# Attention scores made for two key chunks at a time, with the product of the high parts on half the rows

## The chip, the cores and the metric

The kernel runs on one core of one Trainium2 chip. The metric is device time in microseconds (us), the median of the runs of one program; lower is better. All engines of the core work at once: PE is TensorE (matmul), PEld its weight load, DVE is VectorE, ACT is ScalarE, SP the queue that issues the DMAs.

## The reference

Three layers follow each other: an attention with squared ReLU in place of a softmax, a channel mix, and a squared ReLU MLP. The change touches the first alone, in the product of z with itself:

```python
def _attn_ref(u, v, z):                       # u, v: 4 x 3072 x 256, z: 4 x 3072 x 64
    scale = 1.0 / S
    scores = scale * np.matmul(z, z.transpose(0, 2, 1))
    attn = np.maximum(scores, 0.0) ** 2
    out = np.matmul(attn, v)
    return (u * out).astype(np.float32)
```

All inputs are fp32.

## The kernel before

**Numbers in two parts.** Matmuls take fp32r operands. Each fp32 operand is cut into a high part (hi, a rounded copy) and a low part (lo, what is left), and a product is built from three terms, hi by hi, lo by hi and hi by lo, that add up in one PSUM bank.

**z.** z has 64 columns, so its hi and lo parts fit side by side on the 128 partitions. For each batch b and each group g of 512 positions there are two tiles in `zz`: `zhl[b, g]` holds hi on rows 0 to 63 and lo on rows 64 to 127, `zlh[b, g]` holds lo on rows 0 to 63 and hi on rows 64 to 127 (L271 to L275).

**Tiling.** A block n is one batch (4) and one group `ib` of 512 queries (6 of a batch), 24 blocks in all. A step s of a block is one chunk of 128 keys (24 chunks, 4 of a group g). For each step `scores(s)` makes a tile of 128 keys by 512 queries, and `attend(s)` multiplies it by v: six matmuls (L379, L380, L383) that add up over the 24 steps into two PSUM banks. Scores are symmetric: where g < ib the tile comes, turned, from an earlier block by way of DRAM (`turned`, loaded to `mixed`, L336 and L338; taken up by ACT L346 and DVE L347) and no score matmul is issued. So blocks with ib = 0, 1, ... 5 make 24, 20, ... 4 score chunks: 84 in a batch, 336 in all.

**One computed score chunk.** Two matmuls (L351, L352), each over all 128 rows, fill one PSUM bank `sps`: `zhl` by `zhl` gives hi by hi plus lo by lo, `zlh` by `zhl` gives lo by hi plus hi by lo. ACT then applies ReLU (L162, this frees the bank) and the square (L163); hi is made on DVE (L358) or ACT (L356), lo on DVE (L361), and where g > ib DVE transposes the tile for a later block (`turn`, L322), which SP stores.

**Order.** The order is the program's own (nothing is rescheduled). At step s the loop runs what is due by the table `todo` (loads, z and v splits, conversions of weights), then makes scores ahead up to a lead that grows from 4 to 7 steps, then issues `attend(s)`. The pool `ps_w` has four PSUM banks, so the bank of a chunk is the bank of the fourth chunk before it. Each step of the main stretch on PE is thus two score matmuls and six matmuls with v.

Of the kernel before, what the change touches and what calls it, by code (L numbers as in the profile page):

```python
# [7 lines left out]
F32 = mybir.dt.float32  # L8
# [7 lines left out]
P = 128  # L16
Q = 32
T = 512
# [3 lines left out]
def tile_relu2_attention__rwkv_channel_mix__relu2_mlp(  # L22
# [18 lines left out]
    nc = tc.nc  # L41
    B, S, D = u.shape
    DQ = z.shape[2]
# [25 lines left out]
    ps_w = ctx.enter_context(tc.tile_pool(name="ps_w", bufs=4, space=PSUM))  # L69
# [86 lines left out]
    def parts(pool, tag, bufs):  # L156
        return [pool.tile([P, T], F32R, tag=tag + h, name=tag + h, bufs=bufs) for h in ("hi", "lo")]

    def relu2(ps, scale):

        a = el.tile([P, T], F32, tag="a", name="a")
        nc.scalar.activation(out=a, in_=ps, func=AF.Relu, scale=scale)  # L162
        nc.scalar.activation(out=a, in_=a, func=AF.Square)  # L163
        return a
# [77 lines left out]
    def attention():  # L242
        with ExitStack() as st:
# [5 lines left out]
            z_raw, zT, zz, zhl, zlh, vhl, uT = {}, {}, {}, {}, {}, {}, {}  # L249
# [47 lines left out]
                uT[n, d] = io.tile([P, T], F32, tag=f"uT{d}", name="uT", bufs=1)  # L297
                nc.vector.transpose(uT[n, d], raws.pop(("u", n, d)))

            at, acc, ready, staged, late = {}, {}, {}, {}, []  # L300

# [2 lines left out]
            def chunk(s):  # L306

                n, jc = divmod(s, NJ)
                if n % NB == NB - 1:
                    jc = (jc - G) % NJ  # L310
                return n, n // NB, n % NB, jc // G, jc % G
# [6 lines left out]
            def turn(a, i, j, c):  # L318
                if c == 0:
                    staged[i, j] = io.tile([P, R, G, G, Q], F32, tag="turn", name="turn")  # L320
                t, s = staged[i, j], spread[i, j]
                nc.vector.transpose(t[:, :, :, c, :], a.rearrange("x (m r q) -> x q m r" if s else "x (m q r) -> x q m r",  # L322
                                                                  m=G, q=R))
                if c == G - 1:
                    to = turned[i, j]
                    nc.sync.dma_start(out=to if s else to.rearrange("q x f -> x q f"),
                                      in_=t.rearrange("x q m c k -> x q (m c k)"))
# [12 lines left out]
            def scores(s):  # L340
                n, b, ib, g, c = chunk(s)
                if g < ib:
                    a = ready[n, g][:, :, c].rearrange("y p c k -> y c p k")
                    hi, lo = at[s] = parts(*pools["hidden"])
                    hi_v, lo_v = (t.rearrange("y (c p k) -> y c p k", c=G, k=Q) for t in (hi, lo))
                    nc.scalar.copy(hi_v, a)  # L346
                    finish(lambda: nc.vector.tensor_tensor(out=lo_v, in0=a, in1=hi_v, op=ALU.subtract))  # L347
                    return
                cs = slice(c * P, (c + 1) * P)
                ps = ps_w.tile([P, T], F32, tag="w", name="sps")  # L350
                nc.tensor.matmul(ps, lhsT=zhl[b, g][:, cs], rhs=zhl[b, ib], start=True, stop=False)  # L351
                nc.tensor.matmul(ps, lhsT=zlh[b, g][:, cs], rhs=zhl[b, ib], start=False, stop=True)  # L352
                a = relu2(ps, 1.0 / S)
                hi, lo = at[s] = parts(*pools["hidden"])
                if g > ib and s % 3 < 2:
                    nc.scalar.copy(hi, a)  # L356
                else:
                    nc.vector.tensor_copy(hi, a)  # L358
                if g > ib:
                    turn(a, ib, g, c)  # L360
                finish(lambda: nc.vector.tensor_tensor(out=lo, in0=a, in1=hi, op=ALU.subtract))  # L361

            def finish(f=None):

                if late:
                    late.pop()()
                if f:
                    late.append(f)
# [29 lines left out]
            for b in range(1, B):  # L398
                end = b * NB * NJ
                for g in range(NG):  # L400
                    s = end - (46, 44)[g >= NG - 2] + 6 * g
# [3 lines left out]
                    s = end - NJ + G + 5 * g  # L405
# [13 lines left out]
            for n in range(NBLK):  # L419
                s = n * NJ  # L420
# [6 lines left out]
            for n in range(NBLK - 1):  # L427
                b, ib = divmod(n, NB)
                for g in range(ib):
                    need, stored = n * NJ + (g + ib // (NB - 1)) * G - LEAD, (b * NB + g) * NJ + ib * G + G - 1 - FIRST  # L430
                    s = max(need - EARLY, stored + 1, freed[-3] if len(freed) > 2 else 0, taken)
# [37 lines left out]
            s = n_steps - NJ  # L469
# [23 lines left out]
            for s in range(-FIRST, n_steps + 1):  # L493
                for f, a in todo.pop(s, ()):
                    f(*a)
                if made == n_steps:
                    finish()
                while made < min(n_steps, s + 1 + min(LEAD, FIRST + max(0, s - 2 * NJ) // NJ)):
                    scores(made)
                    made += 1  # L500
                if 0 <= s < n_steps:
                    attend(s)
# [320 lines left out]
    with tc.manual_schedule():  # L823
        attention()
        hp = ctx.enter_context(tc.tile_pool(name="hp", bufs=1, reuse_waits="tile"))
        w3 = ctx.enter_context(tc.tile_pool(name="w3", bufs=1, reuse_waits="tile"))
        pools["ops", 0] = ctx.enter_context(tc.tile_pool(name="ops0", bufs=1, reuse_waits="tile"))
        for q in range(2):
            w_tiles(w3, q)
        channel_mix()  # L830
        mlp()
# [29 lines left out]
```

## Time and profile before

| | |
|---|---|
| median of 3 runs | 2539.12 us (2537.5 to 2540.91) |
| the profiled execution, its own time | 2538.36 us |
| its span, first to last instruction | 2536.6 us |
| granted TensorE clock, mean | 0.998 |

The profile is of one execution. "Busy" of PE is the union of its matmuls, whose ends are modelled: a matmul is shown from its start for 0.39 us, though the next may start sooner. So a pace is read from starts. PEld shows the weight loads, one ahead of each matmul. The attention fills the first 980 us of the span; the other two layers, which the change leaves alone, the rest.

### The profile page before, as it was taken

How to read it: one execution, taken by the hardware profiler on the slowest of the kernel's cores; microseconds unless marked ns; L12 is line 12 of the kernel's file. 1: busy time of each engine (PE TensorE's matmuls, PEld its weight loads, DVE VectorE, ACT ScalarE, POOL GpSimd, SP SyncE). 2: the span in 40 equal slices, each digit the busy share in tenths (PEclk: the TensorE clock that was granted, in tenths of full speed). 3: DMA queues.
4: the chain of work that ended last, by engine and by line, in shares of the span. 5: the costliest groups of instructions: out<-in, count | busy, mean ns of one | idle time of the engine just before them, and what ended most of it. 6: DMA issues, size and time to landing. Idle time of an engine off the chain costs nothing.

```text
span 2536.6 us, 31670 instructions
## 1 busy us (share of the span) xinstructions
PE 2513.0 (99%) x11040; PEld 2072.7 (82%) x11040; DVE 2007.8 (79%) x3382; ACT 1664.6 (66%) x2879; POOL 0.2 (0%) x4
## 2 busy tenths in 40 slices
PE   7999999999999999999999999999999999999998
PEld 5888888888888888888888888788888888888887
DVE  8898988988988986777776677877777777777776
ACT  8766876786687654555555566666666666666665
POOL 0000000000000000000000000000000000000000
PEclk9999999999999999999999999999999999999999
DMA  7678677787886770111111112100110011100101
GB/s 189 173 201 202 195 200 186 201 229 185 198 232 185 211 188 26 58 59 42 59 34 50 47 54 67 28 23 17 34 34 17 17 34 34 26 26 17 34 17 17
DMA packets 311121, 243.79 MB, mean 96 GB/s; under 512 B 211377, under 2 KB 229809, under 8 KB 307889
## 3 DMA queue, kind: packets, MB, share of 16 engines
q1 hardware_dynamic: 308848, 241.25, 35.6%
q8 instruction: 86, 1.41, 0.2%
q10 hardware_dynamic: 2112, 0.52, 0.1%
q14 instruction: 75, 0.61, 0.1%
HBM read 136.86 MB, written 104.86 MB: 95 GB/s over the span
## 4 chain that ended last, share of the span: by engine, by line
PE 92%; DVE 3%; ACT 2%; DMA 1%; issue 1%; SPq 1%; DVEq 0%; ACTq 0%
PE ups L652 16%; PE ups L208 13%; PE v L379 9%; PE v L383 9%; PE v L380 9%; PE v L668 6%; PE v L669 6%; PE v L670 6%; PE v L234 3%; PE v L230 3%; PE v L231 3%; PE sps L352 3%; PE sps L351 3%; DMA mixed<-turned 1%; ACT s L692 0%
## 5 line engine op out<-in xcount | busy, mean ns | idle before, releaser
L380 PE MATMUL v<-ahi,vhl 128*128 128x512 f32 x1152 | 448.8, 390 | 2.6 <-DVE vhl L286 2.6
L379 PE MATMUL v<-ahi,vhl 128*128 128x512 f32 x1152 | 449.1, 390 | 1.1 <-ACT ahi L346 1.1
L689 ACT ACTIVATE s<-s 128x512 f32<-128x512 f32 x288 | 181.2, 629 | 333.5 <-DVE s L684 333.4
L383 PE MATMUL v<-alo,vhl 128*128 128x512 f32 x1152 | 356.1, 390 | 4.0 <-DVE alo L361 3.9
L163 ACT ACTIVATE a<-a 128x512 f32<-128x512 f32 x528 | 333.9, 632 | 16.8
L652 PE MATMUL ups<-d,win 128*128 128x512 f32 x1152 | 323.7, 389 | 0.0
L668 PE MATMUL v<-hhi,wout 128*128 128x512 f32 x768 | 299.3, 390 | 0.7 <-ACT hhi L697 0.6
L670 PE MATMUL v<-hlo,wout 128*128 128x512 f32 x768 | 299.3, 390 | 0.5 <-DVE hlo L703 0.5
L669 PE MATMUL v<-hhi,wout 128*128 128x512 f32 x768 | 298.8, 389 | 0.0
L208 PE MATMUL ups<-mixed,wk 128*128 128x512 f32 x1152 | 291.8, 389 | 0.0
L703 DVE TENSOR_TENSOR hlo<-s,hhi 128x512 fp32r<-128x512 f32 x384 | 264.6, 689 | 21.7 <-ACT hhi L697 9.5
L162 ACT ACTIVATE a<-ups 128x512 f32<-128x512 f32 x192 | 114.8, 598 | 235.9 <-PE ups L208 207.9
L383 PEld LDWEIGHTS v<-alo,vhl 128*128 128x128 f32 x1152 | 215.5, 188 | 52.3 <-DVE alo L361 7.9
L380 PEld LDWEIGHTS v<-ahi,vhl 128*128 128x128 f32 x1152 | 216.6, 188 | 48.3 <-DVE vhl L286 3.4
L379 PEld LDWEIGHTS v<-ahi,vhl 128*128 128x128 f32 x1152 | 216.7, 188 | 47.1 <-ACT ahi L346 2.0
L652 PEld LDWEIGHTS ups<-d,win 128*128 128x128 f32 x1152 | 216.3, 188 | 44.9
L208 PEld LDWEIGHTS ups<-mixed,wk 128*128 128x128 f32 x1152 | 216.2, 188 | 44.9
L162 ACT ACTIVATE a<-sps 128x512 f32<-128x512 f32 x336 | 199.2, 593 | 81.5 <-PE sps L352 73.7
L652 PE MATMUL ups<-b,win 128*128 128x512 f32 x864 | 242.9, 389 | 0.0
L692 ACT ACTIVATE s<-s 128x512 f32<-128x512 f32 x384 | 231.2, 627 | 6.1
L322 DVE STREAM_TRANSPOSE turn<-a 128x512 f32<-128x512 f32 x240 | 207.2, 864 | 18.3 <-ACT a L163 16.8
L361 DVE TENSOR_TENSOR alo<-a,ahi 128x512 fp32r<-128x512 f32 x336 | 220.3, 660 | 0.0
(103 smaller groups left out, 3918.0 us busy)
## 6 DMA issues: line engine op xcount, KB each, us to landing
turned<-turn SPq DMA_DIRECT2D x60, 1024.0 KB, 5.1
mixed<-turned SPq DMA_DIRECT2D x220, 256.0 KB, 5.4
raw<-in_v_dram SPq DMA_DIRECT2D x24, 512.0 KB, 4.7
u<-in_u_dram SPq DMA_DIRECT2D x192, 64.0 KB, 4.3
xT<-uT SPq DMA_DIRECT2D x48, 256.0 KB, 2.2
x2d<-xo SPq DMA_DIRECT2D x48, 256.0 KB, 2.2
x<-x2d SPq DMA_DIRECT2D x12, 1024.0 KB, 4.8
out_dram<-y SPq DMA_DIRECT2D x92, 128.0 KB, 2.9
```

What stands on the lines that cost most here:

```text
L162: nc.scalar.activation(out=a, in_=ps, func=AF.Relu, scale=scale)
L163: nc.scalar.activation(out=a, in_=a, func=AF.Square)
L208: nc.tensor.matmul(ps, lhsT=lhs(h, c, f), rhs=rhs[:, m, c, :], start=k == 0, stop=k == 3 * ND - 1)
L379: nc.tensor.matmul(acc[n][d], lhsT=vt[:, 0, c, ds_], rhs=hi, start=first, stop=False)
L380: nc.tensor.matmul(acc[n][d], lhsT=vt[:, 1, c, ds_], rhs=hi, start=False, stop=False)
L383: nc.tensor.matmul(acc[n][d], lhsT=vt[:, 0, c, ds_], rhs=lo, start=False, stop=last)
L652: nc.tensor.matmul(ps, lhsT=win[q][:, h, r, w], rhs=x(y), start=first and m == 0, stop=m == 2, skip_group_check=not first)
L668: nc.tensor.matmul(acc[p, b][d], lhsT=w[:, 0, c, ds_], rhs=hi, start=first, stop=False)
L669: nc.tensor.matmul(acc[p, b][d], lhsT=w[:, 1, c, ds_], rhs=hi, start=False, stop=False)
L670: nc.tensor.matmul(acc[p, b][d], lhsT=w[:, 0, c, ds_], rhs=lo, start=False, stop=last)
L692: nc.scalar.activation(out=tmp[g, c], in_=tmp[g, c], func=AF.Square)
L703: nc.vector.tensor_tensor(out=lo, in0=tmp.pop((g, c)), in1=hi, op=ALU.subtract)
```

## The change

`scores` issues the matmuls of two neighbouring key chunks together, at the even chunk. It takes two PSUM banks and issues four matmuls: for each of the two chunks the cross terms over all 128 rows (`zlh` by `zhl`, L352 of the changed kernel), then for the even chunk hi by hi from rows 0 to 63 (of `zhl`), and for the odd chunk hi by hi from rows 64 to 127 (of `zlh`), both L355. These last two have 64 rows each, and lie on the two halves of the array. The term lo by lo is no longer computed. At the odd chunk no matmul is issued. Everything after the matmuls is as before.

```diff
-            at, acc, ready, staged, late = {}, {}, {}, {}, []
+            at, acc, ready, staged, sps, late = {}, {}, {}, {}, {}, []
...
-                cs = slice(c * P, (c + 1) * P)
-                ps = ps_w.tile([P, T], F32, tag="w", name="sps")
-                nc.tensor.matmul(ps, lhsT=zhl[b, g][:, cs], rhs=zhl[b, ib], start=True, stop=False)
-                nc.tensor.matmul(ps, lhsT=zlh[b, g][:, cs], rhs=zhl[b, ib], start=False, stop=True)
+                if c % 2 == 0:
+                    for k in range(2):
+                        sps[s + k] = ps_w.tile([P, T], F32, tag="w", name="sps")
+                        nc.tensor.matmul(sps[s + k], lhsT=zlh[b, g][:, (c + k) * P:(c + k + 1) * P], rhs=zhl[b, ib],
+                                         start=True, stop=False)
+                    for k, (rows, t) in enumerate(((slice(0, DQ), zhl), (slice(DQ, P), zlh))):
+                        nc.tensor.matmul(sps[s + k], lhsT=t[b, g][rows, (c + k) * P:(c + k + 1) * P],
+                                         rhs=t[b, ib][rows], start=False, stop=True)
+                ps = sps.pop(s)
                 a = relu2(ps, 1.0 / S)
```

On PE, two steps early in the second batch stand in this order before (names: `sps` are the score banks, `v_` or `v0`, `v1` the two banks that add up the product with v, `ahi` and `alo` the parts of a score chunk; numbers are buffers):

```order
L351 MATMUL sps_2860<-zz_1988,zz_2195 128x512 [waits Activation_49]
L352 MATMUL sps_2860<-zz_1988,zz_2195 128x512
L379 MATMUL v0_2730<-ahi_2724,vhl_2532 128x512
L380 MATMUL v0_2730<-ahi_2724,vhl_2532 128x512
L379 MATMUL v1_2731<-ahi_2724,vhl_2532 128x512
L380 MATMUL v1_2731<-ahi_2724,vhl_2532 128x512
L383 MATMUL v0_2730<-alo_2725,vhl_2532 128x512
L383 MATMUL v1_2731<-alo_2725,vhl_2532 128x512
L351 MATMUL sps_2878<-zz_1988,zz_2195 128x512 [waits Activation_49]
L352 MATMUL sps_2878<-zz_1988,zz_2195 128x512
```

After it, the same place on PE (the even chunk's bank has the same name, the odd one's is now `sps_2862`; L384, L385 and L388 are the matmuls with v):

```order
L352 MATMUL sps_2860<-zz_1988,zz_2195 128x512 [waits Activation_49]
L352 MATMUL sps_2862<-zz_1988,zz_2195 128x512 [waits Activation_49]
L355 MATMUL sps_2860<-zz_1988,zz_2195 128x512
L355 MATMUL sps_2862<-zz_1988,zz_2195 128x512
L384 MATMUL v0_2730<-ahi_2724,vhl_2532 128x512
L385 MATMUL v0_2730<-ahi_2724,vhl_2532 128x512
L384 MATMUL v1_2731<-ahi_2724,vhl_2532 128x512
L385 MATMUL v1_2731<-ahi_2724,vhl_2532 128x512
L388 MATMUL v0_2730<-alo_2725,vhl_2532 128x512
L388 MATMUL v1_2731<-alo_2725,vhl_2532 128x512
```

The odd chunk's two matmuls have moved ahead of the even step's six with v, and its wait for ACT (a free bank) with them. The number of matmuls is the same, and the order of the instructions on DVE, ACT and SP has not changed.

## Rows read from the trace of the kernel before

**Rows 1.** The page: span; busy us (share) xinstructions of each engine.

```profile
span 2536.6 us, 31670 instructions
PE 2513.0 (99%) x11040; PEld 2072.7 (82%) x11040; DVE 2007.8 (79%) x3382; ACT 1664.6 (66%) x2879; POOL 0.2 (0%) x4
```

**Rows 2.** Timeline of PE in one step (start us, us, instruction).

```profile
502.24 0.39 PE L351 MATMUL sps<-zz 128*128 128x512 f32 x1
502.46 0.39 PE L352 MATMUL sps<-zz 128*128 128x512 f32 x1
502.69 0.39 PE L379 MATMUL v<-ahi,vhl 128*128 128x512 f32 x1
...
504.05 0.39 PE L351 MATMUL sps<-zz 128*128 128x512 f32 x1
```

**Rows 3.** Timeline of PEld, the weight loads, in the same step.

```profile
502.24 0.19 PEld L352 LDWEIGHTS sps<-zz 128*128 128x128 f32 x1
502.46 0.19 PEld L379 LDWEIGHTS v<-ahi,vhl 128*128 128x128 f32 x1
```

**Rows 4.** What PE, then PEld waited for until 980 us (us, times, longest).

```profile
PE v L383 <- DVE alo L361: 3.9, 7, 0.9
PE v L379 <- ACT ahi L346: 1.1, 2, 0.7
...
PEld v L383 <- DVE alo L361: 7.9, 10, 1.3
PEld v L379 <- ACT ahi L346: 2.0, 2, 1.1
```

**Rows 5.** Stretches: PE, PEld, DVE, ACT, POOL busy us (x), PEclk, DMA share, GB/s.

```profile
12.00:65.20 53.20, 46.60 (x186) 34.77 (x185) 48.58 (x84) 46.48 (x81) 0.00 (x0) 0.97 0.79 204
65.20:106.40 41.20, 41.20 (x183) 34.14 (x182) 34.46 (x62) 32.16 (x55) 0.00 (x0) 1.00 0.71 194
259.70:301.40 41.70, 41.70 (x185) 34.55 (x184) 39.54 (x72) 37.18 (x65) 0.00 (x0) 1.00 0.85 240
301.40:341.30 39.90, 39.90 (x177) 33.04 (x176) 33.29 (x60) 31.03 (x53) 0.00 (x0) 1.00 0.68 191
419.30:457.40 38.10, 38.10 (x170) 31.56 (x169) 33.98 (x62) 24.08 (x42) 0.00 (x0) 1.00 0.82 198
```

**Rows 6.** The source line L352 (xcount: ns min/median/max, first and last start us).

```profile
L352 PE MATMUL sps<-zz x336: 387/389/628, 8.2 to 920.3; 128*128 128x512 f32 x168
```

**Rows 7.** Timeline of PEld, then of PE, just after a wait with the array empty.

```profile
15.27 0.19 PEld L380 LDWEIGHTS v<-ahi,vhl 128*128 128x128 f32 x1 [3.37 <-DVE vhl L286]
15.38 0.19 PEld L379 LDWEIGHTS v<-ahi,vhl 128*128 128x128 f32 x1
...
15.27 0.50 PE L380 MATMUL v<-ahi,vhl 128*128 128x512 f32 x1 [2.65 <-DVE vhl L286]
15.61 0.39 PE L379 MATMUL v<-ahi,vhl 128*128 128x512 f32 x1
```

**Rows 8.** Timeline of ACT: the four ReLUs ahead of 505 us, and the next.

```profile
498.34 0.59 ACT L162 ACTIVATE a<-sps 128x512 f32<-128x512 f32 x1
...
499.50 0.58 ACT L162 ACTIVATE a<-sps 128x512 f32<-128x512 f32 x1
...
501.35 0.60 ACT L162 ACTIVATE a<-sps 128x512 f32<-128x512 f32 x1
...
503.70 0.59 ACT L162 ACTIVATE a<-sps 128x512 f32<-128x512 f32 x1
...
504.86 0.58 ACT L162 ACTIVATE a<-sps 128x512 f32<-128x512 f32 x1
```

**Rows 9.** What ACT waited for until 925 us (us, times, longest).

```profile
ACT a L162 <- PE sps L352: 73.7, 101, 4.4
...
ACT ahi L346 <- DMA mixed<-turned: 31.8, 6, 6.0
```

**Rows 10.** Stretches of 20 us: columns as in rows 5; the last but one is DMA share.

```profile
220.00:240.00 20.00, 20.00 (x90) 16.57 (x89) 17.75 (x31) 11.11 (x20) 0.00 (x0) 1.00 1.05 255
240.00:260.00 20.00, 19.34 (x86) 15.70 (x85) 16.00 (x30) 15.35 (x28) 0.00 (x0) 1.00 0.62 175
```

## The prediction

> **What bounds the kernel now.** The page first: PE is busy 2513 of 2536.6 us, DVE 2008, ACT 1665 [rows 1]. A busy PE need not be a full one, since the ends of matmuls are modelled, so the second view is the timeline of PE in one step. There a matmul starts every 0.23 us, and the eight of the step take 504.05 - 502.24 = 1.81 us, or 0.226 us each [rows 2]. Each weight load starts with the matmul before the one it serves, and is over (0.19 us) before the slot is [rows 3]: loads cost nothing here. The third view is what PE waited for. In the whole attention that is a few us: 7.9 us of its loads for lo on DVE, ten times, and 2.0 us for hi made from turned scores, twice [rows 4]. So PE sets the time, matmul by matmul, at 0.226 us each, and what is taken from PE there is taken from the end, as long as DVE and the DMAs keep up. How far they can is the fourth view, the stretches: a block that begins a batch (ib = 0) has DVE busy 39.5 of 41.7 us, the block after it 33.3 of 39.9, a late one 34.0 of 38.1 [rows 5]. The very first block is another matter: PE is busy 46.6 of 53.2 us there and DVE 48.6, so PE is not what it waits for.
>
> **The change part by part.**
>
> *Matmuls.* There are 336 score chunks [rows 6], so 168 pairs. A pair has four matmuls before and after. Before, they take four slots: 4 x 0.226 = 0.905 us. After, the first two (cross terms, 128 rows) are of the kind that the trace shows: two slots. The other two have 64 rows each, and no matmul of before has less than 128 [rows 6]. They read different rows of SBUF, hold their weights in different rows of the array, and write different banks. If they stream at the same time, the second costs only what it starts late, and that I call d. Its lower bound is 0: nothing else between them is shared. The upper bound of an overlap comes from the weight loads, which share a path. With the array empty a load starts at 15.27 and the next at 15.38 [rows 7], so one load holds the path for 0.11 us. Both loads (0.22 us) just fit into the slot of the second cross matmul, if the second load may run before the first half matmul starts: d = 0. If it starts only with that matmul, as every load does in rows 3, then d = 0.11. The trace has no row between the two, so I take the middle, d = 0.055 us, and keep both ends. A pair then saves 0.226 - 0.055 = 0.171 us.
>
> The Trainium skill speaks on this: "TensorE: Matmul & The Clock Gate", Part 3, The mechanism, says that loads for other row groups are pulled ahead of matmuls, and that matmuls on different row groups start about 4 ns apart. No run here shows it; with 0.004 us for d the sum below would be 2508 us, an estimate.
>
> *Sum.* The 12 pairs of the first block are counted at nothing, since DVE and ACT set its pace [rows 5]. 156 pairs x 0.171 = 26.7 us. From this goes what DVE takes back: in the three later blocks with ib = 0, 12 pairs x 0.171 = 2.1 us bring PE from 41.7 to 39.6 us, and DVE is busy for 39.5 of them [rows 5]; with so little room lo will be late now and then, and I count a third, 0.7 us a block, 2.1 us. And what the DMAs take back: PE already waited twice for turned scores [rows 4], behind ACT, which waited 6.0 us for one such load [rows 9], after a stretch in which the DMA engines were full (share 1.05, then 0.62) [rows 10]. A PE that arrives earlier waits longer there; I count 1.0 us for the four batches. So 26.7 - 2.1 - 1.0 = 23.6 us. The profiled execution has 2538.4 us, so 2514.8; the median of the runs lies 0.8 us above it, so 2516 us. With d = 0 and nothing taken back it is 156 x 0.226 = 35.3 us and 2504, with d = 0.11 it is 156 x 0.116 - 3.1 = 15.0 us and 2524.
>
> *The moved matmuls.* The odd chunk's cross matmul now stands a step ahead, so its bank has to be free a step (1.81 us) earlier. The chunk whose first matmul starts at 504.05 [rows 2] writes the bank that the ReLU from 499.50 to 500.08 freed, four chunks before its own [rows 8]: 3.97 us of room, of which 1.81 - 0.23 = 1.6 go. Behind a PE that waits here the six matmuls with v would queue, and behind them everything; with 2.4 us left I count nothing. The even chunk's ReLU can start one slot (0.23 us) later than now, as its bank is complete with the third matmul in place of the second; the odd one's can start more than a us earlier. ACT waited 73.7 us for scores [rows 9] and is not what bounds; hi and lo of a chunk have four to seven steps until they are used. No cost. The six matmuls with v of the even step start two slots later against their scores, those of the odd step as before: more room for DVE, not less. DVE, ACT and SP do the same work in the same order.
>
> **The rivals.**
>
> *The array has to run empty between matmuls of different depth (slower).* Each pair goes from 128 rows to 64 and back. If the first matmul of the other depth has to wait until the one before has ended, it starts 0.389 us after it [rows 6], not 0.226: 0.163 more, twice a pair. A pair then takes 0.226 + 0.389 + 0.055 + 0.389 = 1.059 us against 0.905, so 0.154 x 168 = 25.9 us more: 2565. If the weight load also has to wait for the empty array, 0.11 more at each switch [rows 7]: 0.374 x 168 = 62.8, 2602. If it is only the load that is no longer hidden, 0.226 + 0.336 + 0.055 + 0.336 = 0.953, 8 us more, 2547. The point from which it decides is 0.171 / 2 = 0.086 us a switch: with more than that the change loses. For it speaks that nothing in the trace shows such a switch, so that nothing shows it free; against it, that in rows 3 and 7 a load never waits for a matmul to end, only for it to start. The Trainium skill has this rule: "TensorEngine Tiling (Array Packing)", Key Properties, says that switching the tiling mode drains TensorE. It gives no price, and no run here shows it.
>
> *The two halves don't run at the same time.* Then d is a whole slot, 0.226, a pair takes what it took, and only the order has changed: 2539, within some us. This is the case in which the change does not do what it says. For it speaks that no two matmuls of before start less than a slot apart.
>
> *The gain is there but DVE or the DMAs take most of it.* In the blocks with ib > 0 that rows 5 show, DVE has 4 to 7 us of room in 38 to 41, and the change takes at most 10 pairs x 0.171 = 1.7 there. For most of the gain to go, DVE would have to be late in all blocks: 2525 to 2533. Unlikely.
>
> **How the numbers follow.** Two runs of this kernel can be told apart from about 0.2% on, 5 us. Forecast, overlap, with 2503 to 2524 as its own range and 2516 as its value: 0.52. Gain mostly taken back: 0.04. No overlap, or a small cost at the switches that eats the gain, 2534 to 2544: 0.13. Slower by the switches, 2545 to 2602: 0.31. So faster 0.56, same 0.13, slower 0.31. Cases of both signs hold much of the chance, so the range is wide: from 2503, below which I leave 0.02, to 2568, above which lies somewhat less than half of the slower case, 0.14.
>
> **What would show it.** In the changed kernel's timeline, the two starts of L355 of one pair: 0 to 0.11 us apart if the halves overlap, 0.23 if they don't. The start of the first L355 after the second L352, and of the next matmul with v after the second L355: 0.23 us each if a switch is free, 0.3 to 0.5 if the array runs empty. The stretch of the attention should end near 980 - 24 = 956 us, and the rest should keep its 1557 us. PE's waits for lo on DVE (7.9 us now) should grow by a few us and no more, and PE should not wait for ACT at L352. The forecast is wrong if the switches cost 0.09 us or more each, or if the second L355 starts a slot after the first.

## The result and the profile after

The change made the kernel slower: 2568.16 us (median of 4 runs, 2567.88 to 2569.05) against 2539.13 us before (4 runs, 2537.5 to 2540.91). The ratio is 1.0115, with a 95% interval of 1.0097 to 1.0132, so 25 to 34 us more. The forecast was 2516 us, faster, with a range up to 2568: wrong in its sign, and just outside its range.

The page of the changed kernel, beside [rows 1]: PE is busy 34 us longer, DVE and ACT are busy as long as before.

```profile
span 2566.3 us, 31723 instructions
PE 2547.4 (99%) x11040; PEld 2029.0 (79%) x11040; DVE 2006.8 (78%) x3382; ACT 1665.5 (65%) x2879; POOL 0.2 (0%) x4
```

Where the time came in is told by the last matmul with v of the attention. Its source line, in the kernel before and in the changed one (name xcount: ns min/median/max, first to last start):

```profile
L383 PE MATMUL v<-alo,vhl x1152: 387/389/628, 16.2 to 980.2; 128*128 128x512 f32 x192
```

```profile
L388 PE MATMUL v<-alo,vhl x1152: 387/390/628, 16.1 to 1009.4; 128*128 128x512 f32 x192
```

The attention ends 29.2 us later, nearly all of the 29.7 us by which the span is longer; what follows takes 2566.3 - 1009.4 = 1556.9 us, against 2536.6 - 980.2 = 1556.4 before. Now one pair of chunks in the changed kernel, the timeline of PE (the L352 row holds both cross matmuls, the L355 row both matmuls of 64 rows):

```profile
504.95 0.61 PE L352 MATMUL sps<-zz 128*128 128x512 f32 x2
505.49 0.50 PE L355 MATMUL sps<-zz 64*128 64x512 f32 x2
505.92 0.50 PE L384 MATMUL v<-ahi,vhl 128*128 128x512 f32 x1
506.26 0.39 PE L385 MATMUL v<-ahi,vhl 128*128 128x512 f32 x1
506.49 0.40 PE L384 MATMUL v<-ahi,vhl 128*128 128x512 f32 x1
```

Two matmuls merged into one row are shown from the start of the first to the modelled end of the last, so a pair a slot apart is 0.226 + 0.39 = 0.61 long (the L352 row). A matmul that finds the array empty is recorded from its weight load on, and is then 0.50 long instead of 0.39; [rows 7] has one such too. The L355 row is 0.50 long for two matmuls: they start together. By single records (each instruction of the trace by itself) it is 0.003 to 0.004 us from the first start to the second, in 168 of 168 pairs. So two matmuls do go in one slot. But look at what is around them. From the start of the first cross matmul (504.95) to the second matmul with v (506.26) it is 1.31 us. Before, the same stretch held four score matmuls and one with v, five slots of 0.226, 1.13 us [rows 2]. One slot fewer, and 0.18 us longer. The loads of the same stretch, timeline of PEld:

```profile
504.72 0.41 PEld L352 LDWEIGHTS sps<-zz 128*128 128x128 f32 x2
505.49 0.19 PEld L355 LDWEIGHTS sps<-zz 64*128 64x128 f32 x2 [0.35 <-issue]
505.92 0.19 PEld L384 LDWEIGHTS v<-ahi,vhl 128*128 128x128 f32 x1 [0.25 <-issue]
506.03 0.19 PEld L385 LDWEIGHTS v<-ahi,vhl 128*128 128x128 f32 x1
```

In [rows 3] each load starts with the matmul before the one it serves. Here the loads of L355 should start with the second cross matmul, at 504.95 + 0.226 = 505.18. They start at 505.49, by single records 0.317 after the second cross matmul, which is a slot and another 0.09. In 165 of the 168 pairs it is 0.317 to 0.327 us. No semaphore held them, the profile says ("issue"). Only then does the load itself run, with nothing streaming: 0.11 us, as the distance of the next two loads shows (506.03 - 505.92). The same stands at the way back: L384's load starts 505.92 - 505.49 = 0.43 us after that of L355, which is 0.11 for the load, 0.226 for the slot, 0.09 again; and the matmul after it follows after 0.34, a slot and 0.11. So a change of depth costs 0.09 + 0.11 = 0.20 us, and a pair has two: 0.40, less the one slot saved, 0.226, is 0.18 us up to the second matmul with v.

The Trainium skill has the rule, "TensorEngine Tiling (Array Packing)", Key Properties: changing the tiling mode drains TensorE. The trace agrees, and puts the price beside it that the page doesn't give. That the 0.09 us are the emptying is the reading by this rule; the trace shows the delay alone.

0.18 us times 168 pairs is 30 us, near the 29.0 measured, but two parts of this sum are off and cancel. By single records five more slots behind each visit take 0.229 to 0.235 us at the median, together 0.02 us a pair; why is open. So a later block with ten pairs takes 43.74 us instead of 41.71, one with eight 41.52 instead of 39.89 (last matmul with v to last matmul with v): 0.203 us a pair. And the first block, whose pace PE doesn't set, is no longer than before: its last matmul with v starts at 63.8 us, before at 64.5. So 156 pairs x 0.203 = 31.7 us, less 0.7 in the first block, less 1.8 by which PE's waits for lo have shrunk (3.9 us in [rows 4], 2.1 now): 29.2, which is what the attention lost.

What PEld, then PE, waited for until 1150 us shows both sides of the visits in sums (us, times, longest), and that the pressure on DVE has not grown: PEld waits 6.9 us for lo, against 7.9 in [rows 4]:

```profile
PEld sps L355 <- issue: 59.9, 168, 0.7
...
PEld v L384 <- issue: 39.3, 160, 0.4
...
PEld v L388 <- DVE alo L366: 6.9, 12, 1.1
...
PE v L388 <- DVE alo L366: 2.1, 5, 0.7
```

### The profile page after: what moved, and what is told of

The parts are those of the page before. It is cut to its first block, busy times and chain, and to the rows that moved or that the text cites. A ratio compares the mean times of both kernels' runs of the same rounds, so it can differ in the third digit from the quotient of the medians.

```text
span 2566.3 us, 31723 instructions
## 1 busy us (share of the span) xinstructions
PE 2547.4 (99%) x11040; PEld 2029.0 (79%) x11040; DVE 2006.8 (78%) x3382; ACT 1665.5 (65%) x2879; POOL 0.2 (0%) x4
## 4 chain that ended last, share of the span: by engine, by line
PE 95%; DVE 2%; ACT 1%; DMA 1%; issue 0%; SPq 0%; DVEq 0%; ACTq 0%
PE ups L657 17%; PE ups L208 13%; PE v L384 11%; PE v L388 10%; PE v L385 10%; PE v L673 6%; PE v L675 6%; PE v L674 6%; PE v L231 3%; PE v L234 3%; PE v L230 3%; PE sps L352 3%; PE sps L355 3%; DMA zn<-in_z_dram 0%; DVE hlo L708 0%
## 5 line engine op out<-in xcount | busy, mean ns | idle before, releaser
L384 PE MATMUL v<-ahi,vhl 128*128 128x512 f32 x1152 | 468.5, 407 | 0.0
L385 PE MATMUL v<-ahi,vhl 128*128 128x512 f32 x1152 | 451.4, 392 | 0.2 <-DVE vhl L286 0.2
L388 PE MATMUL v<-alo,vhl 128*128 128x512 f32 x1152 | 357.8, 392 | 2.4 <-DVE alo L366 2.1
L384 PEld LDWEIGHTS v<-ahi,vhl 128*128 128x128 f32 x1152 | 216.7, 188 | 81.0 <-issue 39.3
L388 PEld LDWEIGHTS v<-alo,vhl 128*128 128x128 f32 x1152 | 215.7, 188 | 52.3 <-DVE alo L366 6.9
L385 PEld LDWEIGHTS v<-ahi,vhl 128*128 128x128 f32 x1152 | 217.2, 189 | 40.7 <-DVE vhl L286 0.7
```

Of the source, the lines that this page charges most:

```text
L384: nc.tensor.matmul(acc[n][d], lhsT=vt[:, 0, c, ds_], rhs=hi, start=first, stop=False)
L385: nc.tensor.matmul(acc[n][d], lhsT=vt[:, 1, c, ds_], rhs=hi, start=False, stop=False)
L388: nc.tensor.matmul(acc[n][d], lhsT=vt[:, 0, c, ds_], rhs=lo, start=False, stop=last)
```

## The experiments

The theory is the one just read: what costs is the *change* of depth, twice a pair, 0.09 us in which nothing starts and a load of 0.11 us that nothing hides. Its rivals: the new order of the matmuls (the odd chunk's brought ahead) costs the time; or the matmul of 64 rows itself does, wherever it stands.

### The order alone

Pairs and order as in the changed kernel, but hi by hi over all 128 rows again:

```diff
-                    for k, (rows, t) in enumerate(((slice(0, DQ), zhl), (slice(DQ, P), zlh))):
-                        nc.tensor.matmul(sps[s + k], lhsT=t[b, g][rows, (c + k) * P:(c + k + 1) * P],
-                                         rhs=t[b, ib][rows], start=False, stop=True)
+                    for k in range(2):
+                        nc.tensor.matmul(sps[s + k], lhsT=zhl[b, g][:, (c + k) * P:(c + k + 1) * P], rhs=zhl[b, ib],
+                                         start=False, stop=True)
```

> The pairing and the order of the changed kernel, but hi by hi over all 128 rows again (with lo by lo, as before), so no matmul has 64 rows. Theory (switch): the loss comes from going from 128 rows to 64 and back, about 0.2 us each time, twice a pair; without 64-row matmuls the time is that of before, 2539 within 5 us. Rival (order): the loss comes from the two banks taken at once and the odd chunk's matmuls moved a step ahead; then about 2568. Rival (half-depth matmul): a 64-row matmul is slow by itself; then 2539 as well.

Measured: 2539.45 us against 2538.12, ratio 1.0007 (0.9997 to 1.0016). Its timeline of PE at the same place:

```profile
507.64 0.62 PE L352 MATMUL sps<-zz 128*128 128x512 f32 x2
508.10 0.61 PE L355 MATMUL sps<-zz 128*128 128x512 f32 x2
508.55 0.39 PE L384 MATMUL v<-ahi,vhl 128*128 128x512 f32 x1
```

Four slots from 507.64 to 508.55, 0.91 us, as before. The order costs 1.3 us at this median, 4 at most by the interval, of 29; that rival is out, and the loss hangs on the depth.

### Both matmuls of 64 rows on the same half

```diff
-                    for k, (rows, t) in enumerate(((slice(0, DQ), zhl), (slice(DQ, P), zlh))):
+                    for k, (rows, t) in enumerate(((slice(0, DQ), zhl), (slice(0, DQ), zhl))):
```

> The changed kernel with both hi by hi products on rows 0 to 63, so that they can't run beside each other. Theory (switch): two changes of depth a pair as in the changed kernel, and the second 64-row matmul one slot (0.226 us) after the first instead of 0.003: 168 x 0.224 = 38 us over 2568, so about 2606. Rival (half-depth matmul): each takes about 0.43 us by itself, so 168 x 0.43 = 72 more, about 2640. Rival (order): 2606 at most, and 2568 if the halves did not overlap anyway.

Measured: 2603.09 us (one run), 34.9 us above the changed kernel.

```profile
514.29 0.61 PE L352 MATMUL sps<-zz 128*128 128x512 f32 x2
514.84 0.73 PE L355 MATMUL sps<-zz 64*128 64x512 f32 x2
515.50 0.50 PE L384 MATMUL v<-ahi,vhl 128*128 128x512 f32 x1
```

The L355 row is now 0.73 long instead of 0.50, a slot more, and L384 comes 0.66 after it instead of 0.43. So in the changed kernel it is the two halves that let the matmuls run together, and that is worth 0.227 us a pair. Behind the first block 156 pairs make 35 us of it, and the first block itself is 0.7 us longer (by single records its last matmul with v starts at 64.5 us, 63.8 in the changed kernel), near the 34.9 measured. The pair's saving is real; the two switches cost nearly twice as much.

### One matmul of 64 rows in every chunk

The kernel before, in its order, with lo by lo left out, so that each chunk goes to 64 rows and back (no pair, nothing saved):

```diff
-                nc.tensor.matmul(ps, lhsT=zhl[b, g][:, cs], rhs=zhl[b, ib], start=True, stop=False)
+                nc.tensor.matmul(ps, lhsT=zhl[b, g][0:DQ, cs], rhs=zhl[b, ib][0:DQ], start=True, stop=False)
```

> The order of the kernel before, one chunk at a time; only the first of the two score matmuls is cut to rows 0 to 63 (hi by hi, lo by lo left out). As many matmuls and slots as before, but two changes of depth for each of the 336 chunks. Theory (switch): 2 x 0.198 us x 336 = 133 us more than before, about 2672. Rival (order): nothing has moved, so 2539. Rival (half-depth matmul, 0.43 us instead of 0.226): 336 x 0.2 = 69 more, about 2608.

Measured: 2664.14 us (one run), 126.0 above the kernel before.

```profile
505.10 0.61 PE L383 MATMUL v<-alo,vhl 128*128 128x512 f32 x2
505.64 0.50 PE L351 MATMUL sps<-zz 64*128 64x512 f32 x1
506.07 0.50 PE L352 MATMUL sps<-zz 128*128 128x512 f32 x1
506.40 0.39 PE L379 MATMUL v<-ahi,vhl 128*128 128x512 f32 x1
```

From 505.10 to 506.40 there are four slots, which is 0.91 us at depth 128 throughout; here it is 1.30. A visit to 64 rows costs 0.39 to 0.40 us. The 312 chunks behind the first block make 122 to 125 us of that, and the first block, whose pace PE doesn't set, is 2.3 us longer (by single records its last matmul with v starts at 66.8 us instead of 64.5): 124 to 127, with 126.0 measured. This is the price of two switches with nothing else in it, 0.20 us each, in an order that is that of the kernel before.

### 96 rows: a smaller depth without a switch

The same line with 96 rows (the term lo by lo is then computed in part):

```diff
-                nc.tensor.matmul(ps, lhsT=zhl[b, g][:, cs], rhs=zhl[b, ib], start=True, stop=False)
+                nc.tensor.matmul(ps, lhsT=zhl[b, g][0:96, cs], rhs=zhl[b, ib][0:96], start=True, stop=False)
```

> The kernel of half_per_chunk with 96 rows in place of 64 in the first score matmul (a part of lo by lo comes in with rows 64 to 95). The built program sets a tile of 128 rows of the array for a matmul of 96 rows, and one of 64 for one of 64. Theory (switch of the tile): no switch, so the time of before, 2539 within 5 us. Rival (any change in the number of rows makes the array run empty): as half_per_chunk, 2664.

Measured: 2545.16 us against 2538.6, ratio 1.0028 (1.0017 to 1.0039).

```profile
505.87 0.40 PE L351 MATMUL sps<-zz 96*128 96x512 f32 x1
506.10 0.40 PE L352 MATMUL sps<-zz 128*128 128x512 f32 x1
506.34 0.40 PE L379 MATMUL v<-ahi,vhl 128*128 128x512 f32 x1
506.57 0.39 PE L380 MATMUL v<-ahi,vhl 128*128 128x512 f32 x1
```

No row of 0.50 here, and no gap of 0.3: fewer rows alone don't bring the delay. What is left is 0.020 us a chunk over these three slots, and by single records 0.027 over four; times the 312 chunks behind the first block that is 8 us, 6.6 was measured. Why these slots are longer no run shows. So the 0.40 is not the price of fewer rows as such: 64 rows have it, 96 have not. That 64 rows are a tile of their own, half the array, and 96 are not, is the reading that the rule above suggests; the runs show only the prices, and no depth but 64, 96 and 128 was run.

### Four chunks at once: half as many switches

Four cross matmuls, then four of 64 rows, in two slots:

```diff
-                if c % 2 == 0:
-                    for k in range(2):
+                if c == 0:
+                    for k in range(G):
...
-                    for k, (rows, t) in enumerate(((slice(0, DQ), zhl), (slice(DQ, P), zlh))):
+                    for k, (rows, t) in enumerate(((slice(0, DQ), zhl), (slice(DQ, P), zlh)) * 2):
```

> The change made for the four chunks of a group at once: four cross matmuls, then four hi by hi, low and high half in turn. Two slots saved and two changes of depth for four chunks. Theory (switch): 84 x (2 x 0.198 - 2 x 0.226) = -5 us, about 2534, plus some us if all four score banks taken at once make PE wait for ACT. Rival (order): the burst is longer and the banks are all taken, so above 2568. Rival (half-depth matmul): the pairs of halves cost what they cost now, so about 2568.

Measured: 2549.94 us against 2538.12, ratio 1.005 (1.0034 to 1.0067).

```profile
507.83 1.12 PE L352 MATMUL sps<-zz 128*128 128x512 f32 x4
508.88 0.73 PE L355 MATMUL sps<-zz 64*128 64x512 f32 x4
509.55 0.50 PE L384 MATMUL v<-ahi,vhl 128*128 128x512 f32 x1
```

The four halves take two slots (0.73 long), with one switch ahead of them and one behind: 0.40 against two slots saved, 0.45, a gain of 0.05 us. Most of that goes in the slots behind, which are longer here too: by single records blocks with five, four and three groups and no wait take 41.75, 39.84 and 38.04 us, before 41.71, 39.89 and 38.08. So two slots saved just pay for the two switches. But the group now takes all four score banks at once, and what it has to wait for is ACT's ReLU, which frees them (waits of PEld, then of PE, until 1000 us; us, times, longest):

```profile
PEld sps L352 <- ACT a L162: 23.7, 25, 3.8
```

```profile
PE sps L352 <- ACT a L162: 15.1, 14, 3.3
```

The kernel before has no such wait. Half of these waits (7.8 us of PE's, 11.5 of PEld's) lie in the first 65 us, where PE doesn't set the pace: the first block is only 0.7 us longer. The others lie nearly all in three blocks, those with ib = 4 of the first three batches; by single records these take 41.1, 41.2 and 41.8 us instead of 38.1, 9.9 us together. In all the attention ends 8.3 us later in the profiled execution, whose own time is 2546.8 us, 8.7 above the kernel before; the median of the four is 11.8 above it. The switches came out as the theory says; the rest is a wait that the changed kernel hardly had.

### The scores wholly in halves

Also the cross terms go in halves, three slots of two matmuls, so that a pair saves a slot as in the changed kernel, with the same two switches:

```diff
...
+                    low, high = slice(0, DQ), slice(DQ, P)
+                    for i, (x, y) in enumerate(((zlh, zhl), (zhl, zlh), (zhl, zhl))):
+                        for k, rows in enumerate((low, high)):
+                            l, r = (x, y) if k == 0 or i < 2 else (zlh, zlh)
+                            nc.tensor.matmul(sps[s + k], lhsT=l[b, g][rows, (c + k) * P:(c + k + 1) * P],
+                                             rhs=r[b, ib][rows], start=i == 0, stop=i == 2)
```

> The pairs of the changed kernel, with the cross terms cut into 64-row matmuls too: the even chunk has its three products on rows 0 to 63, the odd chunk on rows 64 to 127, six 64-row matmuls in three slots. Theory (switch): still two changes of depth a pair, now around all six, and three slots: the same time as the changed kernel, 2568 within 4 us, with a new pair of matmuls every 0.227 us inside. Rival (a 64-row matmul is dear, or its load is not hidden): four more 64-row matmuls a pair, and 0.11 us open for each new pair of loads, 168 x 2 x 0.11 = 36 us more, 2604.

Measured: 2569.27 us (one run), that of the changed kernel.

```profile
505.71 0.97 PE L356 MATMUL sps<-zz 64*128 64x512 f32 x6
506.60 0.50 PE L385 MATMUL v<-ahi,vhl 128*128 128x512 f32 x1
```

Six halves in one row of 0.97: 0.50 for the first pair, after a switch, and two slots of 0.23. Inside the mode the loads are hidden again, and a new pair starts every 0.227 us. Where the switch stands among the score matmuls doesn't matter; how many there are does. This also puts out the second rival: a matmul of 64 rows is not dear wherever it stands, since beside others of 64 rows a pair of them takes the slot of one whole matmul.

### Everything in halves: hardly a switch

If a switch is what costs, the matmuls with v should be in halves too. Each half adds up in a bank of its own (four banks a block in place of two), which ACT and DVE put together at the block's end; the last block stays as before. That is one switch in the whole attention, and 3 slots in place of 4 for each pair, 168 x 0.226 = 38 us less:

```diff
...
+                if n < NBLK - 1:
+                    for i, (h, x) in enumerate(((0, hi), (1, hi), (0, lo))):
+                        for k in range(ND):
+                            for half, d in ((0, k), (1, 1 - k)):
+                                rows = slice(half * DQ, half * DQ + DQ)
+                                nc.tensor.matmul(acc[n][half][d], lhsT=vt[rows, h, c, d * P:(d + 1) * P], rhs=x[rows],
+                                                 start=first and i == 0, stop=last and i == 2)
+                    return
...
+                        nc.scalar.copy(high[d], acc[n][1][d])
...
+                        nc.vector.tensor_tensor(out=high[d], in0=acc[n][0][d], in1=high[d], op=ALU.add)
```

> As scores_halves, and the product with v is cut in halves of 64 keys as well, in all blocks but the last: the two halves add up in banks of their own, four accumulator banks a block, which one copy on ACT and one sum on DVE join at a block's end. So the depth changes once in the whole program. Theory (switch): inside a block two steps with a pair take 15 slots (3.4 us) and no waits between; 38 us fewer on PE than before. At each of 23 block ends PE has to wait until the banks are read, since there is no second set: 0.39 + 0.6 + 0.7 us or more, 35 to 50 us in all. Sum 2535 to 2555; the first part is the test. Rival (64-row matmuls are dear by themselves): the product with v now has 6600 of them, and the attention takes several hundred us more.

Measured: 2587.51 us against 2538.6, ratio 1.0191 (1.0174 to 1.0208). Within a block the pace is what the theory says. A step with v alone has six slots, and starts every 1.36 us:

```profile
500.32 1.07 PE L388 MATMUL v<-ahi,vhl 64*128 64x512 f32 x8
501.22 0.62 PE L388 MATMUL v<-alo,vhl 64*128 64x512 f32 x4
501.68 1.07 PE L388 MATMUL v<-ahi,vhl 64*128 64x512 f32 x8
```

That is 1.36 / 6 = 0.227 for each pair of halves, the 0.226 of a whole matmul. The 38 us are lost elsewhere. What PEld, and PE, waited for between 60 and 960 us:

```profile
PEld v L388 <- DVE high L409: 69.1, 44, 6.1
...
PE v L388 <- DVE high L409: 51.1, 22, 5.6
```

A block has all four banks, so the next one can't start until ACT and DVE have emptied them. And a wait costs twice. Two stretches (PE, PEld, DVE, ACT, POOL busy us, granted clock, DMA share, GB/s); in the second such a wait of 1.7 us ends, at 319.52:

```profile
300.00:318.00 18.00, 17.84 (x158) 14.43 (x154) 15.44 (x29) 13.98 (x25) 0.00 (x0) 1.00 0.82 219
318.00:328.00 10.00, 8.38 (x58) 6.70 (x60) 8.07 (x15) 6.27 (x12) 0.00 (x0) 0.83 0.33 81
```

The granted clock is 0.83 there, some of the stretch at the lower of the two levels (1.2 and 2.4 GHz). Over the span it is 0.987, against 0.998 before, which is worth some 29 us (0.011 x 2591.5, an estimate). Waits of 51.1 to 69.1 us and 29 of clock, less 38 saved, give 42 to 60 us more; 48.9 was measured, 54.7 in the profiled execution.

### Smaller waits at the block's end

Three kernels try to shorten that. In the first (all_64b) the last step of a block ends one bank early, the first step starts with it, and the order of the copies follows:

```diff
-                            for half, d in ((0, k), (1, 1 - k)):
...
+                    if first or last:
+                        order = [(i, d) for d in range(ND) for i in range(3)]
```

> all_64 with a shorter wait at block ends: in the first and the last step of a block the matmuls go by output half (both row halves of the first output half, then of the second), and the sum of each output half waits for one ACT copy instead of two. Theory (switch, with the accumulator banks as the only new bound): 38 us fewer on PE than in the kernel before; the wait at a block's end falls from 2.05 us to 0.4 + 0.6 + 0.7 - 0.7 - 0.2 = 0.8 us, over 22 block ends 18 us instead of 69 in all, plus some us at the three block ends where ACT is behind; and with shorter waits the granted clock should stay at full. Sum 2515 to 2530, faster than before. Rival (64-row matmuls or their many loads cost something that the waits hid): no faster than before, 2540 or more, with PE full.

In the second (all_64c) the last step of a block and the copies go ahead of the other work of that step:

```diff
...
+                if early:
+                    attend(s)
+                    gate(s // NJ, 0)
                 for f, a in todo.pop(s, ()):
...
```

> all_64b with the reading of the accumulator banks put ahead of the other ACT and DVE work of the last step of a block, so that it does not stand behind casts that wait for something else. Theory (switch, and the accumulator banks as the new bound): in all_64b PE still waited 56 us at block ends, 7 us each at three blocks where ACT was behind; these should fall to 0.8 to 1.5 us each, 20 to 30 us in all, and the clock stay nearer to full: 2520 to 2540. Rival (the matmuls over half the rows cost something of their own): the waits fall and the time stays above 2555.

Measured: 2565.38 us against 2538.06, ratio 1.0105 (1.0088 to 1.0122), and 2544.57 against 2537.9, 1.0027 (1.0017 to 1.0038). Their waits, first all_64b, then all_64c:

```profile
PEld v L392 <- DVE high L413: 56.4, 23, 7.5
```

```profile
PEld v L392 <- DVE high L413: 37.3, 30, 5.9
```

With 69.1, 56.4 and 37.3 us of waits the three kernels stand 48.9, 27.3 and 6.7 us above the kernel before. From the first to the second the time falls by more than the waits, as it should if each wait also costs clock: the profiled executions were granted 0.987, 0.995 and 0.997. In the last one the longest waits that are left, 4.3 to 5.9 us by single records, lie at the ends of three late blocks (ib = 4), where ACT and DVE have other work queued; at most other blocks' ends it is about 1.1 us.

### Halves only where ACT and DVE have room

In the first three blocks of a batch (ib = 0 to 2) everything is in halves, in the others all is 128 deep, in pairs: 7 switches, and 108 pairs that save a slot, 24 us. The second kernel (mixed_64b) also brings forward the end of the block before a block of halves:

```diff
+            def halves(n):
+                return n % NB < 3 and n < NBLK - 1
```

> The halves only where they pay: the first three blocks of a batch (ib = 0, 1, 2: many score chunks) run wholly in 64-row matmuls, with four accumulator banks, as in all_64c; the last three (few score chunks) wholly in 128-row matmuls, with two banks in turn, as in the kernel before. The depth changes 7 times in the program; 108 pairs are made of halves. Theory (switch and accumulator banks): 108 x 0.226 = 24 us fewer on PE; 12 block ends with a wait of 0.3 to 1.1 us, 4 to 13 us; the long waits of all_64c at the ends of blocks with ib = 4 (5.5 us) gone. Sum 11 to 20 us less than before: 2518 to 2528, faster than both kernels. Rival (something else in the 64-row matmuls costs, as their loads): no faster than before, 2538 or more.

```diff
+            def ahead(n):
+                return halves(n) or halves(n + 1)
...
-                early = 0 <= s < n_steps and s % NJ == NJ - 1 and halves(s // NJ)
+                early = 0 <= s < n_steps and s % NJ == NJ - 1 and ahead(s // NJ)
```

> mixed_64 with one more edit: at the end of the three blocks with ib = 5 that a block of halves follows, the accumulators are read ahead of the other ACT and DVE work of that step. In mixed_64 the block after each took 46 to 47.7 us instead of 41.7, with a wait of 5 us for that reading at its start. Theory (switch and accumulator banks): the wait falls to about 1.5 us as in all_64c, and those blocks to 40 us: 18 to 22 us less than mixed_64, 2522 to 2530, faster than before. Rival (the blocks of halves are slow for another reason): the wait falls and the blocks stay above 42 us, 2536 or more.

Measured: 2545.8 us against 2537.77, ratio 1.0029 (1.0017 to 1.004), and 2536.56 against 2538.36, 0.9994 (0.9985 to 1.0003), not told apart from the kernel before. What PEld waited for in the one, then in the other:

```profile
PEld v L402 <- DVE uT L430: 15.0, 3, 5.3
...
PEld v L402 <- DVE high L423: 6.6, 9, 1.2
```

```profile
PEld v L405 <- DVE uT L433: 8.4, 3, 3.1
PEld v L405 <- DVE high L426: 6.8, 10, 1.2
```

The block ends inside the halves are now short. What is left is the passage from two banks to four at the start of a batch, where DVE is fullest [rows 5]. One such passage in mixed_64b, stretch by stretch (columns as above):

```profile
256.00:260.00 4.00, 1.56 (x7) 0.78 (x5) 4.00 (x9) 3.91 (x8) 0.00 (x0) 0.91 0.43 133
260.00:264.00 4.00, 3.60 (x18) 2.82 (x20) 4.00 (x8) 1.97 (x4) 0.00 (x0) 0.50 0.35 131
```

PE does 1.56 us of work in 4 us, DVE and ACT are busy throughout, and the next four microseconds have a clock of 0.50, the lower level (1.2 GHz). The waits of the two rows (8.4 and 6.8 us) and the clock behind them take back much of the 24 us; where the rest of them goes is not shown. No version beats the kernel before by more than can be measured. Halves that add up in one bank were not tried.

## Why the prediction was wrong

**The step that failed** is in the paragraph *Matmuls*: both loads "just fit into the slot of the second cross matmul". That was read from [rows 3] and [rows 7], which have loads of one depth only, and it was carried over to a change of depth. The trace of the changed kernel has those loads 0.317 us after the second cross matmul's start, within 0.01 us of that in all but three pairs, and the run with 64 rows in each chunk shows the same delay in the order of the kernel before, and six halves in a row show it only at their two ends: it is the change of depth that does it. The sum had no term for a switch at all: 2 x 0.20 x 156 = 62 us in the pairs that it counted, against 35 saved.

**What held.** The halves overlap: d was put between 0 and 0.11 and is 0.003, at the lower end, since the two loads start as close together as the matmuls and don't take turns at 0.11 us each, as the upper bound had it. So the gain of the overlap by itself was sized too small (0.171 a pair in place of 0.223). The Trainium skill's "TensorE: Matmul & The Clock Gate", Part 3, The mechanism, has about 4 ns between two such starts, and the trace agrees with 3 to 4. The moved matmuls cost nothing, as the run of the order alone shows, and PEld waited for ACT at L352 once, for 0.8 us. The rest of the kernel kept its 1557 us, and the 12 pairs of the first block, counted at nothing, changed nothing there. DVE took back nothing, since PE came later and not earlier.

**The rivals.** The slower rival is what happened, with 0.31. It was named with its mechanism, its place and a point from which it decides, 0.086 us a switch; with d = 0.003 that point lies at 0.11, and the switch costs 0.20. Its three prices were each wrong in a part. The one that had the load wait too, 2602, is the right mechanism, but the delay ahead of the load was put at 0.163, the rest of a matmul's shown length after its slot, and is 0.09; and d at 0.055. With 0.09 and 0.003 in its own formula a pair takes 0.226 + (0.226 + 0.20) + 0.003 + (0.226 + 0.20) = 1.08 us, 0.18 above the 0.905, and over 168 pairs the time is 2569, with the two parts that cancel as said above. The one without the open load gave 2565, near the measured time by luck: the delay and d were put too high and the load left out, and these errors cancel. The load starts 0.09 us after the slot, not 0.163: the modelled end of a matmul is not the time from which the next load can start.

**The weighing.** "Nothing in the trace shows such a switch, so that nothing shows it free" was the right sentence; after it the argument against the switch was taken from rows of another kind. With a decision point of 0.09 us and bounds from 0 to 0.27 a switch, most of the bounds lay on the slower side, and the chances should have too.

## What to carry to other kernels

Running two small matmuls on two parts of the array saves a slot, but going to the other tile size and back costs two switches: here 0.40 us against 0.23, so a visit that saves two slots breaks about even, and one that saves more pays, unless it takes banks that other engines must first empty. Count the changes of tile size in the order of PE's instructions before counting the matmuls. Where the trace of the old kernel has no row of the new kind, the forecast belongs between the bounds, not at the end that rows of the old kind suggest.

## What was not expected of the hardware

A matmul of 96 rows among those of 128 is not free, though it brings no delay ahead of its load: 0.23 to 0.24 us for the four slots from it on, 0.027 us a chunk. Two matmuls on the two halves have their loads 3 to 4 ns apart in the changed kernel, so that a pair of halves has the pace of one whole matmul (0.227 us), loads and all. And a wait on PE, 2.8 us long in mixed_64b, cost more than itself: the clock granted in the 4 us behind it was 0.50.
